# An attention, expert and spatial-gating kernel on one core: first loads reordered, table products and decayed queries of the first chunks moved between engines

## The chip, the cores and the metric

The kernel runs on one core of a Trainium2 chip. The metric is the device time of one execution in microseconds (us), lower is better; the core's engines TensorE, VectorE, ScalarE and GpSimd work side by side, each through its own queue in order, and SyncE (SP) issues most DMAs.

## What is computed

Three stages follow each other: a linear attention with decay, a mixture of experts, and a gated feed-forward with a spatial product. The change touches the attention alone:

```python
def _attn_ref(r, k, v, w, u):                 # B, H, S, D = 2, 8, 768, 48
    state = np.zeros((B, H, D, D))
    for t in range(S):
        kt, vt, rt = k[:, :, t], v[:, :, t], r[:, :, t]
        cur = np.einsum('bhd,bhe->bhde', u[None] * kt, vt)
        y[:, :, t] = np.einsum('bhd,bhde->bhe', rt, state + cur)
        state = w[None, :, :, None] * state + np.einsum('bhd,bhe->bhde', kt, vt)
    return y
...
x = attention.transpose(0, 2, 1, 3).reshape(B, S, H * D)   # then:
# moe: each token goes to one of 8 experts (argmax of x @ w_gate, or the expert of the token before
#      it where a local gate says so); out = p[e] * (relu(x @ w1[e]) @ w2[e])
# moe2: u, v = halves of relu(x @ w_in); out = (u * (w_spatial @ norm(v) + b_spatial)) @ w_out
```

## The kernel before

**Chunks.** The 768 time steps are cut into 6 chunks of 128 (`NC`, `C`), each with 2 batches; I write (c,b) for chunk and batch, and the kernel numbers such halves g = 2c + b. Inside a chunk the recurrence is done as matrix products. A table `rtab` holds the powers of w, `ktab` their reciprocals; queries times `rtab` (tile `rh`) and keys times `ktab` (tile `kt`) give `scores` on TensorE (PSUM tile `pa`, two tiles, one buffer each), `mask` (VectorE) keeps the strictly earlier keys (`am`), and `mix` adds up on TensorE the state of the chunk before (`py` from `st`, L625) and the values under the mask (`py`, L630), after making the new state (`pst`, L614, one PSUM buffer, added into `st` by VectorE, L619, or copied, L621). `prep_keys` makes the keys for the state, `kh` (GpSimd), from `ktok`, the transposed table that `tokens_table` makes: product `one0` (trace: `one`) on VectorE with `wc`, four transposes `pk` on TensorE, a copy on ScalarE.

**Gates and own weights.** `gates` copies v into `vx` on ScalarE, has TensorE multiply it with the gate weights (`gated`, tile `pg`, one PSUM buffer; for (0,0) the buffer `py0`) and copies `pg` into `vx` on ScalarE. `diag` is a generator of three steps: k times u (L546) and times r (L548) on GpSimd (`ku`), and the sum of these over each head on VectorE (`ad`, L551). `own` multiplies `vx` by `ad`, eight instructions on ScalarE (`av`, L567); `own_gates`, `logits` and `rows` read it on VectorE. `decay` multiplies the state by `wc` on ScalarE (L599).

**Order.** The whole is written under a manual schedule: each engine works its instructions off in the order in which the program issues them, and waits on semaphores where one needs another's result or buffer. So the order of the calls in L701 to L748, and in the loop from L748 on (c = 1 to 4), is the order of each queue. `warm` (L101) issues products of constants on TensorE before the first data are there.

**Loads.** `load(c, names, b)` issues one DMA a tensor, for one batch or both, all on SP's queue; the tiles have two buffers a name. Chunk 0 and chunk 1 are issued at L428 to L438, chunk 2 in L725, chunks c + 2 in the loop. `kT`, `rT`, `vT` hold channels in the partitions, `k`, `r`, `v` time steps. `wgb` are the gate weights, `ub` is u for all partitions.

**Who does which product.** `prep` (L503): for (0,0) `powers` makes the tables on VectorE and, in `ready`, two halves of `kt` as the table grows; then GpSimd makes `rh`. Else `kt` is made by VectorE for (0,1), all of chunk 1 and (c,0) of chunks 2 to 4, and by GpSimd otherwise; `rh` is made by GpSimd throughout (L515, L518). `wc` is computed by VectorE at the end of `powers` (L484), `wBad` (a check of w's range) at L736.

Of the kernel before, what the change touches and what calls it, by code (L numbers as in the profile page):

```python
# [16 lines left out]
ALU = mybir.AluOpType  # L17
# [4 lines left out]
B = 2  # L22
# [7 lines left out]
C = 128  # L30
NC = S // C
# [5 lines left out]
G = E + 1  # L37
WS = 3072
LC = D + G
WARM = (16, 9)  # L40
FILL = (3, 0, 0, 7, 0, 1, 0, 5)
WMIN = 0.6
WMAX = 1.1
# [3 lines left out]
def rwkv_moe_gmlp(ctx, tc, a, out):  # L47
# [53 lines left out]
    def warm(ps, tag, n):  # L101

        t = ps.tile([128, 4, 128], F32, name="warm", tag=tag)
        for _ in range(n):
            pe.matmul(t, lhsT=ones, rhs=ones.unsqueeze(1).to_broadcast([128, 4, 128]), start=True, stop=True)
# [301 lines left out]
    with ExitStack() as att:  # L407
# [6 lines left out]
        wT = tp.tile([128, NP], F32, name="wT")  # L414
# [6 lines left out]
        def load(c, names, b=slice(0, B)):  # L421
            t = loads.setdefault(c, {})
            for n in names:
                if n not in t:
                    t[n] = ld.tile(shapes[n], F32, name=n, tag=n)
                sy.dma_start(out=t[n][:, b], in_=a[n][c, :, b])

        wgb = tp.tile([128, 3, H * G], F32, name="wgb")  # L428
        sy.dma_start(out=wgb, in_=a["wgb"])
        load(0, ["vT", "rT", "kT"], 0)  # L430
        load(0, ["vT", "rT", "kT"], 1)
        load(0, ["v", "k"])
        ub = tp.tile([128, H, D], F32, name="ub")
        sy.dma_start(out=ub.rearrange("t h d -> t (h d)"), in_=a["u"].partition_broadcast(128))
        load(0, ["r"])
        for b in range(B):
            load(1, ["kT", "rT", "vT"], b)
        load(1, ["v", "k", "r"])  # L438

        zero = tp.tile([128, DM], F32, name="zero")  # L440
        st = [tp.tile([128, B, NP, C], F32, name=f"st{i}") for i in range(2)]
# [3 lines left out]
        def clear(i):  # L445
            def z(*shape):
                t = zero[:, 0:shape[-1]]
                for _ in shape[:-1]:
                    t = t.unsqueeze(1)
                return t.to_broadcast([128, *shape])  # L450

            v = vx[i].rearrange("t b p a d -> t (b p) a d")
            se.copy(v[:, :, 0, LC:C], z(B * NP, C - LC))
            se.copy(v[:, :, 1, 0:D], z(B * NP, D))
            se.copy(v[:, :, 1, D + LC:C], z(B * NP, C - LC - D))
            se.copy(kh[i][:, :, :, D:64], z(B, H, 64 - D))
            se.copy(st[1 - i].rearrange("t b p d -> t (b p) d"), z(B * NP, C))
# [9 lines left out]
        def powers(ready):  # L467

            ve.memset(one0, 0.0)
            ve.memset(one0[:, :, 0:1], 1.0)  # L470
            ve.memset(wrep[:, :, 0:1], 0.0)

            ve.tensor_scalar(wrep[:, :, 1:C], wT.unsqueeze(2).to_broadcast([128, NP, C - 1]), WMIN, WMAX,
                             op0=ALU.max, op1=ALU.min)
            ve.tensor_tensor_scan(out=flat(rtab), data0=flat(wrep), data1=flat(one0),
                                  initial=0.0, op0=ALU.mult, op1=ALU.add)
            ve.reciprocal(ktab[:, :, 0:16], rtab[:, :, 1:17])
            n = 16
            while n < C:
                ve.tensor_tensor(ktab[:, :, n:2 * n], ktab[:, :, 0:n],  # L480
                                 ktab[:, :, n - 1:n].to_broadcast([128, NP, n]), op=ALU.mult)
                n *= 2
                ready(n)
            ve.tensor_tensor(wc, rtab[:, :, C - 1], wrep[:, :, 1], op=ALU.mult)  # L484

        ktok = tp.tile([128, H, D], F32, name="ktok")

# [15 lines left out]
        def prep(c, b):  # L503

            t = loads[c]
            rh[c, b] = wk.tile([128, NP, C], F32, name="rh", tag=f"rh{b}")
            kt[c, b] = wk.tile([128, NP, C], F32, name="kt", tag=f"kt{b}")
            if c + b == 0:
                def ready(n):
                    o = slice(n // 2, n) if n == C else slice(0, n)  # L510
                    if n >= C // 2:
                        ve.tensor_tensor(kt[0, 0][:, :, o], t["kT"][:, 0, :, o], ktab[:, :, o], op=ALU.mult)

                powers(ready)
                po.tensor_tensor(rh[0, 0], t["rT"][:, 0], rtab, op=ALU.mult)  # L515
                return
            (ve if c * b < 2 and c < NC - 1 else po).tensor_tensor(kt[c, b], t["kT"][:, b], ktab, op=ALU.mult)
            po.tensor_tensor(rh[c, b], t["rT"][:, b], rtab, op=ALU.mult)  # L518

        def prep_keys(c, b=slice(0, B)):  # L520
            k = loads[c]["k"][:, b]
# [3 lines left out]
        def gated(c, b, tag="pg"):  # L525

            pg = ps1.tile([128, H, G], F32, name="pg", tag=tag)
            for k in range(3):
                pe.matmul(pg.rearrange("t h g -> t (h g)"), lhsT=loads[c]["vT"][:, b, k, :],  # L529
                          rhs=wgb[:, k, :], start=(k == 0), stop=(k == 2))  # L530
            return pg
# [47 lines left out]
        def scores(g):  # L579

            c, b = divmod(g, B)
            am[g] = wk.tile([128, 2 * NP, C], F32, name="am", tag="am")
            pa = [ps1.tile([128, NP, C], F32, name="pa", tag=f"pa{h}") for h in range(2)]

            for p in range(NP):
                for h in range(2):
                    pe.matmul(pa[h][:, p, :], lhsT=kt[c, b][64 * h:64 * h + 64, p, :],  # L587
                              rhs=rh[c, b][64 * h:64 * h + 64, p, :], start=True, stop=True)
            am[g, "pa"] = pa
# [109 lines left out]
            sy.dma_start(out=xd[r:r + C, :], in_=x.rearrange("t h d -> t (h d)"))  # L699

        with tc.manual_schedule():  # L701
            warm(ps1, "pz", WARM[0])
            board = Board(ps1, sm)
            pg = gated(0, 0, "py0")
            warm(ps1, "pz", WARM[1])
            prep(0, 0)
            scores(0)
            clear(0)
            tt = tokens_table()
            next(tt)  # L710
# [15 lines left out]
            mask(1)  # L726
            y0 = mix(0)
            prep(1, 0)
            prep(1, 1)
            prep_keys(1)  # L730
            y1 = mix(1)
            next(dg)
            gates(1, 0)
            own(0, 0)
            scores(2)
            ve.tensor_tensor(wBad, wT, wrep[:, :, 1], op=ALU.not_equal)  # L736
            mask(2)
            load(3, ["kT", "rT"])
            own_gates(0, 0)
            logits(0, 0, y0)  # L740
            rows(0, 0, y0)
            gates(1, 1)
            own(0, 1)
            old = rt = iter(())
# [2 lines left out]
            next(dg)  # L747
            for c in range(1, NC - 1):  # L748
                if c + 2 < NC:
                    load(c + 2, [n for n in shapes if n not in loads.get(c + 2, ())])  # L750
                if c < 3:
                    sy.dma_start(out=whole[:, :, 512 * c - 512:512 * c], in_=w_part(0, c - 1))
                if c > 1:
                    w_fetch(*((0, c) if c < NF else (1, 0)))
                next(rt, 0)
                scores(B * c + 1)
                next(dg)
                decay(c, 0)
                mask(B * c + 1)
                prep(c + 1, 0)  # L760
                prep(c + 1, 1)
                if c == 1:
                    own_gates(0, 1)
                    logits(0, 1, y1)
                gates(c + 1, 0)
                decay(c, 1)
                if c + 2 < NC:
                    prep_keys(c + 1)
                next(rt, 0)
                own(c, 0)  # L770
                y0 = mix(B * c)
                rows(c - 1, 1, y1)
                next(rt, 0)
                next(rt, 0)
                own_gates(c, 0)
                scores(B * c + 2)
                gates(c + 1, 1)
                dg = diag(c + 1)
                next(dg)
                next(dg)  # L780
                logits(c, 0, y0)
                rows(c, 0, y0)
                next(old, 0)
                own(c, 1)
                if c == 3:
                    w_split(0, 2, po)

                def selected():
                    next(rt, 0)
                    next(rt, 0)  # L790
                    mask(B * c + 2)

                def ranked():
                    next(rt, 0)
                    next(old, 0)

                y1 = mix(B * c + 1, {0: selected, 2 if c == NF else 3: ranked})
                own_gates(c, 1)
                if c < NF:
                    logits(c, 1, y1)  # L800
                if c == 1:
                    pw_ = ps1.tile([128, NP], F32, name="pwb", tag="pg")
                    pe.matmul(pw_, lhsT=ones, rhs=wBad, start=True, stop=True)
                    ve.tensor_reduce(limit[:, E:E + 1], pw_, axis=AX.X, op=ALU.max)
                if c < NF:
                    old, rt = rt, iter(())
                    if place[c][1] == len(place[c][0]) - 1:
                        g = place[c][0]
                        rt = route(g, board, xr[g, "l"], als[g], sm, ps1)
# [688 lines left out]
```

## Time and profile before

| what | value |
|---|---|
| median of 3 timed runs | 362.3 us (362.19 to 363.47) |
| the profiled execution | 364.96 us |
| its span, first to last instruction | 363.3 us |
| TensorE (PE) busy | 351.5 us, 97% of the span |
| VectorE (DVE) busy | 230.4 us, 63% |
| ScalarE (ACT) busy | 175.8 us, 48% |
| GpSimd (POOL) busy | 171.1 us, 47% |
| mean granted clock of TensorE | 0.990 of full speed |
| attention, experts, spatial stage (by the chain) | 0 to about 80, to about 219, to 363 us |

Times are in us from the start of the span. PE is the matrix product, PEld the weight load that overlaps it. An instruction's duration includes time for which it holds its engine while something blocks it. "[1.59 <-DVE kt L517]" behind an instruction says how long its engine sat idle before it and whose work ended that. The ends of matrix products are modelled, and a group with x16 is 16 instructions from the first start to the last end. L numbers are lines of the kernel.

### The profile page before, as it was taken

To read this page: it belongs to the slowest core of one execution; us is meant where nothing else is said; L and a number is where in the kernel's file an instruction comes from. 1 tells how busy PE (TensorE), PEld (TensorE's weight loads), DVE (VectorE), ACT (ScalarE), POOL (GpSimd) and SP (SyncE) were. 2 spreads that over 40 slices of the span, in tenths; PEclk is the share of its full clock that TensorE was granted. 3 is DMA by queue.
4 is the path that set the end of the run, shared out by engine and by line. 5 is a ranking of instruction groups with operands and counts; after the bars stand their busy time and mean duration, and the time that the engine had idled before them with its cause. 6 is when DMAs were issued, how large, how long until landed. Compare 5 with 4: busy or idle time off the path is not lost.

```text
span 363.3 us, 6486 instructions
## 1 busy us (share of the span) xinstructions
PE 351.5 (97%) x2488; PEld 335.7 (92%) x2488; DVE 230.4 (63%) x428; ACT 175.8 (48%) x344; POOL 171.1 (47%) x106
## 2 busy tenths in 40 slices
PE   8898999999999999999999999999999999999993
PEld 3897999988999999999999999788999999999992
DVE  5867898896569689898988652466787233234000
ACT  4477466652587674746564442345568210102321
POOL 4799993938489773829291023441000522322000
PEclk9998999999999999999999999999999999999997
DMA  6999988233799999988898303436211000000322
GB/s 195 367 405 398 399 266 332 62 114 109 213 357 318 312 334 345 312 275 302 291 307 267 131 1 93 147 95 219 79 19 70 2 0 0 3 0 3 110 87 73
DMA packets 35496, 67.27 MB, mean 185 GB/s; under 512 B 2752, under 2 KB 19392, under 8 KB 35456
## 3 DMA queue, kind: packets, MB, share of 16 engines
q1 hardware_dynamic: 33520, 61.07, 48.8%
q0 software_dynamic: 1792, 5.51, 4.9%
q8 instruction: 21, 0.34, 0.4%
q10 hardware_dynamic: 144, 0.20, 0.2%
q14 instruction: 19, 0.16, 0.1%
HBM read 56.54 MB, written 10.22 MB: 184 GB/s over the span
## 4 chain that ended last, share of the span: by engine, by line
PE 84%; DVE 4%; POOL 4%; DMA 3%; ACT 2%; issue 1%; SPq 0%; POOLq 0%; ACTq 0%; DVEq 0%
PE h L1011 17%; PE o L1061 15%; PE vs L1178 14%; PE po L1194 7%; PE v L1124 7%; PE u L1163 5%; PE py L630 4%; PE pa L587 3%; PE tx L929 2%; PE py L625 2%; PE pst L614 2%; PE pg L529 2%; PE h L1040 2%; DMA kT<-kT 1%; PE o L667 1%
## 5 line engine op out<-in xcount | busy, mean ns | idle before, releaser
L346 POOL TENSOR_TENSOR slot<-raw,slot 128x1536 fp32r<-128x1536 f32 x17 | 61.4, 3612 | 88.8 <-ACT slot L344 88.6
L1011 PE MATMUL h<-xt,slot 128*128 128x256 f32 x504 | 61.7, 284 | 0.0
L1011 PEld LDWEIGHTS h<-xt,slot 128*128 128x128 f32 x504 | 61.3, 192 | 0.1
L1061 PE MATMUL o<-slot,ht 128*128 128x384 f32 x336 | 60.2, 336 | 0.0
L1061 PEld LDWEIGHTS o<-slot,ht 128*128 128x128 f32 x336 | 57.9, 188 | 0.0
L346 DVE TENSOR_TENSOR slot<-raw,slot 128x1536 fp32r<-128x1536 f32 x19 | 42.8, 2253 | 17.4 <-ACT slot L344 17.4
L344 ACT CAST slot<-raw 128x1536 fp32r<-128x1536 f32 x36 | 53.1, 1477 | 0.0
L1178 PE MATMUL vs<-slot,slot 128*128 128x384 f32 x288 | 50.1, 334 | 0.0
L1178 PEld LDWEIGHTS vs<-slot,slot 128*128 128x128 f32 x288 | 49.9, 188 | 0.0
L1185 ACT CAST slot<-gv 128x768 fp32r<-128x768 f32 x8 | 6.7, 837 | 43.9 <-POOL gv L1184 39.4
L1124 PE MATMUL v<-slot,xT 128*128 128x512 f32 x108 | 27.6, 401 | 0.0
L402 POOL DMA_INDIRECT xe<-xd,rowid x16 | 23.7, 1478 | 7.0 <-DVE count L257 3.1
L1184 POOL TENSOR_TENSOR gv<-gv,uT 128x768 f32<-128x768 f32 x7 | 12.9, 1836 | 28.0 <-DVE gv L1182 28.0
L1163 PE MATMUL u<-xT,slot 128*128 128x384 f32 x144 | 25.4, 336 | 0.2 <-ACT uT L1168 0.2
L1163 PEld LDWEIGHTS u<-xT,slot 128*128 128x128 f32 x144 | 25.0, 188 | 0.6 <-ACT uT L1168 0.5
L1194 PE MATMUL po<-slot,slot 128*128 128x384 f32 x144 | 25.1, 335 | 0.0
L630 PE MATMUL py<-vx,am 128*128 128x128 f32 x192 | 25.1, 279 | 0.0
L1194 PEld LDWEIGHTS po<-slot,slot 128*128 128x128 f32 x144 | 25.0, 188 | 0.0
L1021 DVE SCALAR_TENSOR_TENSOR ht<-h,ht 128x512 fp32r<-128x512 f32 (+1 forms) x28 | 18.0, 647 | 8.4 <-ACT ht L1020 8.4
L1124 PEld LDWEIGHTS v<-slot,xT 128*128 128x128 f32 x108 | 19.5, 189 | 3.7
L919 POOL DMA_INDIRECT xg<-ys,slots x12 | 12.0, 1000 | 23.1 <-DMA ys<-ob 14.7
L630 PEld LDWEIGHTS py<-vx,am 128*128 128x128 f32 x192 | 22.9, 192 | 0.0
(205 smaller groups left out, 553.7 us busy)
## 6 DMA issues: line engine op xcount, KB each, us to landing
raw<-w SPq DMA_DIRECT2D x30, 768.0 KB, 6.5
raw<-w_in SPq DMA_DIRECT2D x6, 768.0 KB, 6.3
ys<-ob SPq DMA_DIRECT2D x15, 192.0 KB, 5.0
v<-v SPq DMA_DIRECT2D x6, 384.0 KB, 6.9
k<-k SPq DMA_DIRECT2D x6, 384.0 KB, 7.4
r<-r SPq DMA_DIRECT2D x6, 384.0 KB, 7.7
xd<-x SPq DMA_DIRECT2D x12, 192.0 KB, 3.4
raw<-w_out SPq DMA_DIRECT2D x3, 768.0 KB, 4.5
```

What stands on the lines that cost most here:

```text
L344: se.copy(hi, r)
L346: (eng or ve).tensor_tensor(lo, r, hi, op=ALU.subtract)
L402: po.indirect_dma_start(out=xe[e][:, m], out_offset=None, in_=xd[0:rows_read], in_offset=bass.IndirectOffsetOnAxis(ap=rowid[:, m, e:e + 1] ...
L630: pe.matmul(y[:, p], lhsT=m[:, h * NP + p, :], rhs=v[:, b, p, h, :], start=(c + p + h == 0), stop=(p == NP - 1 and h == 1))
L1011: pe.matmul(h[:, j], lhsT=w1[:, s, k, 128 * f:128 * f + 128], rhs=xt[e][:, m, k], start=(n == 0), stop=(n == 8))
L1021: ve.scalar_tensor_tensor(lo, x, 0.0, hi, op0=ALU.max, op1=ALU.subtract)
L1061: pe.matmul(o, lhsT=hidden(e, m, s, f), rhs=w2[:, q, f], start=(n == 0), stop=(n == 23))
L1124: pe.matmul(o, lhsT=xT[b][:, s, k, 128 * c:128 * c + 128], rhs=win[:, q, k, DF:FF], start=(n == 0), stop=(n == 8))
L1163: pe.matmul(o[:, h, 0:HS], lhsT=win[:, s, k, 128 * d:128 * d + 128], rhs=xT[b][:, q, k, HS * h:HS * h + HS], start=(n == 0), stop=(n == 8))
L1178: pe.matmul(o[:, h, 0:HS], lhsT=vn[b][:, s, k, 128 * d:128 * d + 128], rhs=wsp[q][:, k, HS * h:HS * h + HS], start=(n == 0), stop=(n == 17))
L1184: (ve if b == 1 and d == 3 else po).tensor_tensor(t, t, uT[b][:, d], op=ALU.mult)
L1194: pe.matmul(o, lhsT=gt[b][:, s, k, 128 * c:128 * c + 128], rhs=wout[q][:, k], start=(n == 0), stop=(n == 11))
```

## The change

The first loads come in the order wT, kT and rT of (0,0), wgb, vT of (0,0), then kT, rT, vT of (0,1); chunk 1 is loaded whole, without a split by batch, and kT, rT, vT of chunk 5 are split. `wc` is computed right behind the scan. `rh` of (0,0), (0,1), (1,0), (1,1) and (2,0) is made by VectorE, the rest stays with GpSimd; who makes `kt` is the same as before in another form. 24 warming products come in one piece and `gated(0, 0)` behind `scores(0)`. The sum `ad` of chunk 0 is made between the products of (1,0) and (1,1), `own(0, 0)` stands ahead of `gates(1, 0)`, `wBad` behind `rows(0, 0)`, and the sum `ad` of chunk 1 behind mask(3) and the products of chunk 2.

```diff
--- before.py
+++ after.py
@@ -37,7 +37,7 @@
 G = E + 1
 WS = 3072
 LC = D + G
-WARM = (16, 9)
+WARM = 24
 FILL = (3, 0, 0, 7, 0, 1, 0, 5)
 WMIN = 0.6
 WMAX = 1.1
@@ -425,17 +425,16 @@
                     t[n] = ld.tile(shapes[n], F32, name=n, tag=n)
                 sy.dma_start(out=t[n][:, b], in_=a[n][c, :, b])
 
+        load(0, ["kT", "rT"], 0)
         wgb = tp.tile([128, 3, H * G], F32, name="wgb")
         sy.dma_start(out=wgb, in_=a["wgb"])
-        load(0, ["vT", "rT", "kT"], 0)
-        load(0, ["vT", "rT", "kT"], 1)
+        load(0, ["vT"], 0)
+        load(0, ["kT", "rT", "vT"], 1)
         load(0, ["v", "k"])
         ub = tp.tile([128, H, D], F32, name="ub")
         sy.dma_start(out=ub.rearrange("t h d -> t (h d)"), in_=a["u"].partition_broadcast(128))
         load(0, ["r"])
-        for b in range(B):
-            load(1, ["kT", "rT", "vT"], b)
-        load(1, ["v", "k", "r"])
+        load(1, list(shapes))
 
         zero = tp.tile([128, DM], F32, name="zero")
         st = [tp.tile([128, B, NP, C], F32, name=f"st{i}") for i in range(2)]
@@ -474,6 +473,7 @@
                              op0=ALU.max, op1=ALU.min)
             ve.tensor_tensor_scan(out=flat(rtab), data0=flat(wrep), data1=flat(one0),
                                   initial=0.0, op0=ALU.mult, op1=ALU.add)
+            ve.tensor_tensor(wc, rtab[:, :, C - 1], wrep[:, :, 1], op=ALU.mult)
             ve.reciprocal(ktab[:, :, 0:16], rtab[:, :, 1:17])
             n = 16
             while n < C:
@@ -481,7 +481,6 @@
                                  ktab[:, :, n - 1:n].to_broadcast([128, NP, n]), op=ALU.mult)
                 n *= 2
                 ready(n)
-            ve.tensor_tensor(wc, rtab[:, :, C - 1], wrep[:, :, 1], op=ALU.mult)
 
         ktok = tp.tile([128, H, D], F32, name="ktok")
 
@@ -512,10 +511,9 @@
                         ve.tensor_tensor(kt[0, 0][:, :, o], t["kT"][:, 0, :, o], ktab[:, :, o], op=ALU.mult)
 
                 powers(ready)
-                po.tensor_tensor(rh[0, 0], t["rT"][:, 0], rtab, op=ALU.mult)
-                return
-            (ve if c * b < 2 and c < NC - 1 else po).tensor_tensor(kt[c, b], t["kT"][:, b], ktab, op=ALU.mult)
-            po.tensor_tensor(rh[c, b], t["rT"][:, b], rtab, op=ALU.mult)
+            else:
+                (ve if (c < 2 or b == 0) and c < NC - 1 else po).tensor_tensor(kt[c, b], t["kT"][:, b], ktab, op=ALU.mult)
+            (ve if 2 * c + b < 5 else po).tensor_tensor(rh[c, b], t["rT"][:, b], rtab, op=ALU.mult)
 
         def prep_keys(c, b=slice(0, B)):
             k = loads[c]["k"][:, b]
@@ -699,12 +697,11 @@
             sy.dma_start(out=xd[r:r + C, :], in_=x.rearrange("t h d -> t (h d)"))
 
         with tc.manual_schedule():
-            warm(ps1, "pz", WARM[0])
+            warm(ps1, "pz", WARM)
             board = Board(ps1, sm)
-            pg = gated(0, 0, "py0")
-            warm(ps1, "pz", WARM[1])
             prep(0, 0)
             scores(0)
+            pg = gated(0, 0, "py0")
             clear(0)
             tt = tokens_table()
             next(tt)
@@ -726,19 +723,19 @@
             mask(1)
             y0 = mix(0)
             prep(1, 0)
+            next(dg)
             prep(1, 1)
             prep_keys(1)
             y1 = mix(1)
-            next(dg)
+            own(0, 0)
             gates(1, 0)
-            own(0, 0)
             scores(2)
-            ve.tensor_tensor(wBad, wT, wrep[:, :, 1], op=ALU.not_equal)
             mask(2)
             load(3, ["kT", "rT"])
             own_gates(0, 0)
             logits(0, 0, y0)
             rows(0, 0, y0)
+            ve.tensor_tensor(wBad, wT, wrep[:, :, 1], op=ALU.not_equal)
             gates(1, 1)
             own(0, 1)
             old = rt = iter(())
@@ -747,6 +744,9 @@
             next(dg)
             for c in range(1, NC - 1):
                 if c + 2 < NC:
+                    if c + 2 == NC - 1:
+                        load(c + 2, ["kT", "rT", "vT"], 0)
+                        load(c + 2, ["kT", "rT", "vT"], 1)
                     load(c + 2, [n for n in shapes if n not in loads.get(c + 2, ())])
                 if c < 3:
                     sy.dma_start(out=whole[:, :, 512 * c - 512:512 * c], in_=w_part(0, c - 1))
@@ -754,12 +754,14 @@
                     w_fetch(*((0, c) if c < NF else (1, 0)))
                 next(rt, 0)
                 scores(B * c + 1)
-                next(dg)
+                if c > 1:
+                    next(dg)
                 decay(c, 0)
                 mask(B * c + 1)
                 prep(c + 1, 0)
                 prep(c + 1, 1)
                 if c == 1:
+                    next(dg)
                     own_gates(0, 1)
                     logits(0, 1, y1)
                 gates(c + 1, 0)
```

## Rows read from the trace of the kernel before

**Rows 1.** Busy us, share of the span and instructions, from the page.
```profile
PE 351.5 (97%) x2488; PEld 335.7 (92%) x2488; DVE 230.4 (63%) x428; ACT 175.8 (48%) x344; POOL 171.1 (47%) x106
```
**Rows 2.** Timeline of TensorE: start, us, engine, line, instruction, [idle before, releaser].
```profile
1.13 5.24 PE L105 MATMUL warm<-ones 128*128 128x512 bf16 x16 [1.13 <-DVE ones L71]
6.20 0.79 PE L529 MATMUL pg<-wgb,vT 128*128 128x72 f32 x6
6.83 2.11 PE L105 MATMUL warm<-ones 128*128 128x512 bf16 x9
9.52 1.16 PE L587 MATMUL pa<-rh,kt 64*128 64x128 f32 x16 [0.59 <-DVE kt L512]
...
12.63 1.66 PE L587 MATMUL pa<-rh,kt 64*128 64x128 f32 x16
...
21.50 0.89 PE L529 MATMUL pg<-wgb,vT 128*128 128x72 f32 x6
...
30.16 1.16 PE L587 MATMUL pa<-rh,kt 64*128 64x128 f32 x16 [1.59 <-DVE kt L517]
```
**Rows 3.** Windows: length, PE busy (instructions), PEclk (granted clock), DMA share, GB/s.
```profile
29.00:30.00 1.00, 0.00 (x0) 1.00 1.02 407
...
32.00:33.00 1.00, 1.00 (x6) 0.50 1.03 397
```
**Rows 4.** The chain of work that ended last: start, us, what.
```profile
2.67 5.39 DMA kT<-kT
...
37.40 1.09 PE pa L587 x16
...
39.30 0.33 PE pz L186 x4
...
43.34 1.09 PE pa L587 x16
```
**Rows 5.** Timeline of VectorE.
```profile
8.16 0.42 DVE L512 TENSOR_TENSOR kt<-kT,ktab 128x256 f32<-128x256 f32 x1 [1.40 <-DMA kT<-kT]
...
9.29 1.26 DVE L484 TENSOR_TENSOR wc<-rtab,wrep 128x4 f32<-128x4 f32 x1
10.59 0.69 DVE L489 TENSOR_TENSOR one<-ktab,wc 128x512 f32<-128x512 f32 x1
...
16.93 2.30 DVE L517 TENSOR_TENSOR kt<-kT,ktab 128x512 f32<-128x512 f32 x1
...
20.09 0.95 DVE L551 TENSOR_REDUCE ad<-ku 128x16 f32<-128x768 f32 x1
...
27.05 0.95 DVE L551 TENSOR_REDUCE ad<-ku 128x16 f32<-128x768 f32 x1 [3.12 <-POOL ku L548]
...
37.67 0.20 DVE L167 TENSOR_TENSOR board<-board,als 128x36 f32<-128x36 f32 x1
```
**Rows 6.** Timeline of GpSimd.
```profile
9.26 1.26 POOL L518 TENSOR_TENSOR rh<-rT,rtab 128x512 f32<-128x512 f32 x1 [1.38 <-DMA rT<-rT]
12.58 1.96 POOL L522 TENSOR_TENSOR kh<-k,ktok 128x384 f32<-128x384 f32 x2 [2.05 <-ACT ktok L494]
14.50 1.82 POOL L546 TENSOR_TENSOR ku<-k,ub 128x768 f32<-128x768 f32 x1
16.39 2.28 POOL L548 TENSOR_TENSOR ku<-ku,r 128x768 f32<-128x768 f32 x1
```
**Rows 7.** Timeline of ScalarE.
```profile
21.07 1.97 ACT L567 ACTIVATE av<-vx,ad 128x57 f32<-128x57 f32 x8 [0.29 <-DVE ad L551]
22.95 0.50 ACT L536 COPY vx<-v 128x384 f32<-128x384 f32 x1
23.48 0.23 ACT L538 COPY vx<-pg 128x72 f32<-128x72 f32 x1
```
**Rows 8.** SP issues k of chunk 1; below it that DMA's time from issue to landing.
```profile
14.07 0.33 SPq L426 DMA_DIRECT2D k<-k  x1
...
k<-k SPq DMA_DIRECT2D x1, 384.0 KB, 6.4
```

## Prediction, made before the changed kernel was run

> **What bounds the kernel now.** I read the busy shares first: TensorE works 97% of the span [rows 1], so a change can only bring what TensorE idles or does at a lower clock. Its timeline says where that is: idle stretches ahead of scores(0) (0.59 us) and of scores(4), the first scores of chunk 2 (1.59 us, the largest of the whole run, ended by VectorE's kt), and a scores(1) of 1.66 us where scores(0) took 1.16, so 0.5 of it is waiting [rows 2]. The windows show what followed the 1.59: TensorE did nothing from 29 to 30, and from 32 to 33 its granted clock was 0.50, that is 1.2 instead of 2.4 GHz [rows 3]. The chain of waits gives the price: scores(4) to scores(5) is 37.40 - 30.16 = 7.24; the next half chunk is 43.34 - 37.40 = 5.94 with 0.33 of routing in it. At full clock the first would have been about 5.6; the low clock cost 1.6 [rows 2, 4]. From there the chain is nearly all TensorE. So the question is when scores(4) starts, and at what clock its neighbourhood runs.
>
> Why is scores(4) late? VectorE sat idle 3.12 ahead of ad(1), waiting for GpSimd's ku; mask(3) and kt(2,0) queue behind ad(1) [rows 5]. GpSimd worked without a pause from 12.58, when ktok let its kh begin [rows 6].
>
> I write (c,b) for chunk and batch; scores and masks are numbered 2c+b.
>
> **The start.** kt(0,0) waited 1.40 for kT, issued at 2.67 and landed 5.39 later [rows 4, 5]. In first place kT is issued near 1.3. The wgb and vT that stood there (300 KB) had landed by 6.20, when TensorE read them without a wait [rows 2]; so 256 KB land by then at the latest, and VectorE needs them at 8.16 - 1.40 = 6.76. The 1.40 goes. wc moves forward; it took 1.26, nearly all of it behind GpSimd's rh(0,1), which began at 9.26 and took as long [rows 5, 6]. Behind the scan GpSimd is idle, so its price lies between 0 and the 0.20 of a 36-column product [rows 5]; I take 0.20. kt(0,0) then begins at 6.96, and where wc stood before (1.13 on) VectorE can begin rh(0,0): 8.09. That is an addition: 0.69, as the product of the same size at 10.59 [rows 5]. scores(0) starts 0.15 behind it, at 8.93 instead of 9.52. The 24 warming products end at about 6.4 + 8 x 0.23 = 8.2 [rows 2], ahead of it, so they cost nothing.
>
> VectorE goes on with one, kt(0,1) and rh(0,1) at about 0.65 each: mask(0) starts at 10.7. TensorE does scores(0) to 10.1 and, now in this place, pg(0,0) (0.79) to 10.9; only then the table's transposes. From the end of one to kh there were 12.58 - 11.28 = 1.30 [rows 5, 6], so kh starts at about 12.15, 0.43 earlier. TensorE gains more: 0.4 at scores(1) and its 0.5 of waiting.
>
> **Chunk 1: turns between VectorE and GpSimd.** The second kt of chunk 1 took 2.30 instead of 0.69: it started at 16.93, while GpSimd's ku ran from 16.39, and ended 0.56 after that (16.39 + 2.28 = 18.67). That ku itself took 2.28, not 1.82, having waited 0.46 for the first kt [rows 5, 6]. So such products take turns. The Trainium skill, GPSIMD Engine Reference, section Specifications, says that GpSimd's SBUF interfaces are shared with VectorE and contended when VectorE's instruction has two SBUF inputs; this speaks against the change, whose rh have two, and the trace agrees with its 2.30. Without any contention ad(0) below would come 0.9 earlier and the forecast would be 360.1; the row decides, and I keep the turns.
>
> GpSimd: kh 1.92, ku 1.82, to 15.9; then kt(1,0) has a turn, then ku times r, to 18.67 - 0.43 = 18.24. rh(1,0), now VectorE's, waits for that and ends at 18.8; ad(0) takes 0.95, own(0,0) can start at 19.8. So of the two rh that GpSimd loses in chunk 1 (1.26 each [rows 6]) VectorE makes good use only in part.
>
> own(0,0) now stands ahead of gates(1,0) on ScalarE. Queued behind it are the copies of v and pg; own took 1.88 to the next start (21.07 to 22.95), the copy of v 0.53 to the next start and that of pg 0.23 [rows 7]. pg(1,0) is thus copied out at 19.8 + 1.88 + 0.53 + 0.23 = 22.4, and pg(1,1), which uses the same PSUM buffer, can start only then: at 22.45, against 21.50 before [rows 2]. TensorE is there at 21.50 - 0.9 = 20.6: a **new wait of 1.8 us**. Before, pg(1,1) to the end of mix(2) was 28.57 - 21.50 = 7.07, with 0.5 of waiting for mask(2) that now goes. TensorE is through at 22.45 + 6.57 = 29.0.
>
> **The other way to scores(4).** ad(1) no longer stands ahead of mask(3), so the 3.12 is off this path; kt(2,0) and the added rh(2,0) are on it. GpSimd cannot begin kh(1) before k(1) lands, 14.07 + 6.4 = 20.5 [rows 8]; the bytes ahead of it in the queue are the same as before. kt(1,1) and rh(1,1) follow ad(0) to 21.0; kh(1) takes the next turn, and three of 1.82 end at 26.5; kt(2,0) 27.0; GpSimd's kt(2,1) 1.27, 28.3; rh(2,0) 28.85. Both ways meet at **29.0, 1.15 us before the old 30.16**.
>
> Moves at nothing: wBad behind rows, where a lost turn lies ahead of mask(3) but ends with GpSimd's second ku, some 0.5 before mask(3) is needed; uncovered it costs up to 1.8. ad(1) behind rh(2,0): own(1,0) and the adds into st come later; mix(3) waits about 0.25 for the PSUM buffer, if TensorE is at full clock. Whole loads of chunk 1 make kt(1,0) wait for 512 KB, hidden behind ku. The three more DMA issues for chunk 5 lie in SP's queue some 15 us ahead of use. The relief of GpSimd in chunk 2 is off the path.
>
> **Sum and clock.** The old wait of 1.59 was followed by the low clock. The new one of 1.8 is of that size, with TensorE as busy around it, so I take it that the clock falls again, now within chunk 1, at the same 1.6. Nothing then waits long at scores(4), and no second fall comes. Old and new fall cancel: scores(4) 29.0 + 1.6 = 30.6, scores(5) 36.2 against 37.40, a gain of 1.2; up to 0.3 of the low stretch lies beside waits that are there anyway. Gain 1.3. The profiled execution took 364.96 with a span of 363.3, of which 1.3 would leave 363.7 and 362.0; the median of the timed runs, 362.3, is 2.7 below it, and I take the gain from that: **361.0**. Its own bounds (wc, the turn of kt(1,0), the 0.3) are +-0.8: 360.2 to 361.8.
>
> **Rivals.**
> - *The clock stays up.* The new wait is followed by the low clock in nothing that the trace shows yet, and shorter idle stretches (0.59 at 9.5) were not. Then scores(5) comes at 29.0 + 5.6 + 0.25 = 34.85, a gain of 2.6: 359.7. The timed runs of before spread by 1.3 us, which may be the same thing the other way round.
> - *Lost turns: slower.* rh(2,0) reaches scores(4) with 0.15 to spare, so each further turn that VectorE loses on this path is paid in full. If k(1) lands before 20.3, kh(1) goes ahead of rh(1,1): 1.6 later, 362.6, already slower than before. If then mask(3) ends behind GpSimd's ku, kt(2,0) or rh(2,0) loses one more: 364.2. It decides at k(1)'s landing; 20.5 speaks against it, narrowly.
> - *It brings nothing.* The loads hold chunk 1 anyway: k(1) is 20.5 whatever GpSimd is relieved of, and if whole loads land 1 us later than their halves did, ad(0) and pg(1,1) slip by as much and the gain is gone: 362.3.
>
> **How the numbers follow.** Forecast 0.43, clock up 0.32, lost turns 0.13 (0.08 for one, 0.05 for two), nothing 0.12. The range reaches from below the second to above one lost turn: 359.2 to 363.0. A measurement of this kernel tells about 0.5% (1.8 us) from no change. Faster than 360.5: nearly all of the second and a fifth of the first, 0.40; slower than 364.1: two lost turns and a little, 0.06; between, 0.54.
>
> **What would show it.** scores(0) near 8.9 with no wait for kT; kh at 12.1; ad(0) ending near 19.8; TensorE waiting before pg(1,1), ended by ScalarE's copy at 22.4; scores(4) near 29.0 and no wait of VectorE ahead of mask(3); a granted clock of 0.50 for about 3 us somewhere from 24 on (forecast) or none (rival). I am wrong if ad(0) is done before 18 (own(0,0) then ends before pg(1,0) is there, and nothing waits at pg(1,1)), or if TensorE stops somewhere behind 37.

## The result: 367.0 us against 362.4, and the profile after

The changed kernel takes **367.01 us** (365.80 to 367.75) against 362.4 of the kernel before; the ratio is 1.0106, with an interval of 1.0068 to 1.0143. It is slower by about 1.1%, where 361.0 was forecast.

| | before | after |
|---|---|---|
| median of timed runs | 362.4 us | 367.01 us |
| traced execution, its span | 364.96, 363.3 us | 365.80, 363.5 us |
| TensorE, VectorE, GpSimd busy | 351.5, 230.4, 171.1 us | 353.0, 231.7, 165.0 us |

The two traced executions lie only 0.8 apart: of the 80 executions of the kernel before that were run beside the experiments, 58 had a mean granted clock of 0.994 or more and a median of 362.4 us, and 22 had 0.992 or less and a median of 364.7; the traced one, at 0.990, is like the latter, and all four of the changed kernel had 0.981 to 0.988.

The waits of TensorE in the changed kernel (engine, tile and line, what ended it: us, times, longest):

```profile
PE pg L527 <- ACT vx L536: 2.0, 1, 2.0
...
PE pa L585 <- DVE rh L516: 0.4, 1, 0.4
```

The wait of 1.59 ahead of scores(4) [rows 2] is gone, and a new one of 1.96 stands ahead of pg(1,1), ended by ScalarE. TensorE's timeline (columns as in rows 2):

```profile
8.74 1.16 PE L585 MATMUL pa<-rh,kt 64*128 64x128 f32 x16 [0.38 <-DVE rh L516]
...
22.13 1.56 PE L527 MATMUL pg<-wgb,vT 128*128 128x72 f32 x6 [1.96 <-ACT vx L536]
23.62 2.08 PE L585 MATMUL pa<-rh,kt 64*128 64x128 f32 x16
...
26.97 2.01 PE L612 MATMUL pst<-vx,kh 128*128 128x128 f32 x8
...
33.22 1.16 PE L585 MATMUL pa<-rh,kt 64*128 64x128 f32 x16
...
38.75 1.16 PE L585 MATMUL pa<-rh,kt 64*128 64x128 f32 x16
```

pg(1,1) took 1.56 where a pg took 0.89 [rows 2], and pst 2.01. The windows say why (length, PE busy, PEclk, DMA share, GB/s):

```profile
21.00:22.00 1.00, 0.00 (x0) 1.00 1.04 415
22.00:23.00 1.00, 0.87 (x4) 0.52 1.01 399
...
27.00:28.00 1.00, 1.00 (x6) 0.50 1.00 398
...
31.00:32.00 1.00, 1.00 (x7) 0.50 1.04 402
...
33.00:34.00 1.00, 1.00 (x17) 1.00 1.02 372
```

The granted clock fell at the end of the wait and stayed at 0.50 to a little after 32, about 10 us, with TensorE busy in every one of these windows. In the kernel before it was low for about 3, from shortly before 32 [rows 3] to shortly after 35:

```profile
34.00:35.00 1.00, 1.00 (x6) 0.50 1.02 367
35.00:36.00 1.00, 1.00 (x11) 0.93 1.05 388
```

scores(5), at 37.40 before [rows 4], is at 38.75.

What ended the wait can be read along ScalarE and VectorE (timelines), and from SP's issue of k of chunk 1 with that DMA's time to landing:

```profile
19.44 1.97 ACT L565 ACTIVATE av<-vx,ad 128x57 f32<-128x57 f32 x8 [3.96 <-DVE ad L549]
21.32 0.50 ACT L534 COPY vx<-v 128x384 f32<-128x384 f32 x1
21.85 0.23 ACT L536 COPY vx<-pg 128x72 f32<-128x72 f32 x1
```

```profile
15.64 2.31 DVE L515 TENSOR_TENSOR kt<-kT,ktab 128x512 f32<-128x512 f32 x1 [0.73 <-DMA kT<-kT]
17.87 0.68 DVE L516 TENSOR_TENSOR rh<-rT,rtab 128x512 f32<-128x512 f32 x1
18.47 0.94 DVE L549 TENSOR_REDUCE ad<-ku 128x16 f32<-128x768 f32 x1
19.33 0.68 DVE L515 TENSOR_TENSOR kt<-kT,ktab 128x512 f32<-128x512 f32 x1
19.93 0.68 DVE L516 TENSOR_TENSOR rh<-rT,rtab 128x512 f32<-128x512 f32 x1
...
21.47 1.29 DVE L591 TENSOR_TENSOR am<-pa,upst 128x512 f32<-128x512 f32 x2
```

```profile
19.90 2.38 POOL L520 TENSOR_TENSOR kh<-k,ktok 128x768 f32<-128x768 f32 x1 [2.51 <-DMA k<-k]
```

```profile
10.53 0.33 SPq L426 DMA_DIRECT2D k<-k  x1
...
k<-k SPq DMA_DIRECT2D x1, 384.0 KB, 9.3
```

own(0,0) began when ad(0) was there, the copies of v and pg of (1,0) came behind it, and pg(1,1) behind these. GpSimd's kh(1) is seen to begin 0.03 ahead of rh(1,1) and yet took 2.38, where a product of that size took 1.81 or 1.82 otherwise, and rh(1,1) its plain 0.68: here VectorE still had the turn.

### The profile page after: what moved, and what is told of

Same layout as the page of the kernel before. It is cut to its first block, busy times and chain, and to the rows that moved or that the text cites. A ratio compares the mean times of both kernels' runs of the same rounds, so it can differ in the third digit from the quotient of the medians.

```text
span 363.5 us, 6477 instructions
## 1 busy us (share of the span) xinstructions
PE 353.0 (97%) x2487; PEld 337.7 (93%) x2487; DVE 231.7 (64%) x433; ACT 175.7 (48%) x344; POOL 165.0 (45%) x101
## 4 chain that ended last, share of the span: by engine, by line
PE 86%; DMA 4%; DVE 4%; ACT 2%; SPq 2%; issue 1%; POOL 0%; POOLq 0%; ACTq 0%
PE h L1013 17%; PE o L1063 15%; PE vs L1180 14%; PE po L1196 7%; PE v L1126 7%; PE u L1165 5%; PE py L628 4%; PE pa L585 3%; PE py L623 2%; PE pg L527 2%; PE tx L931 2%; PE pst L612 2%; DMA kT<-kT 2%; PE h L1042 2%; SPq L426 1%
## 5 line engine op out<-in xcount | busy, mean ns | idle before, releaser
L628 PE MATMUL py<-vx,am 128*128 128x128 f32 x192 | 25.9, 285 | 0.0
L565 ACT ACTIVATE av<-vx,ad 128x57 f32<-128x57 f32 x88 | 21.7, 331 | 5.5 <-DVE ad L549 5.5
L628 PEld LDWEIGHTS py<-vx,am 128*128 128x128 f32 x192 | 23.8, 199 | 0.0
```

The source lines that it names most:

```text
L565: se.mul(av[c, b][:, h], v[:, b, h // 2, h % 2, o:o + LC], ad[c][:, b, h:h + 1])
L628: pe.matmul(y[:, p], lhsT=m[:, h * NP + p, :], rhs=v[:, b, p, h, :], start=(c + p + h == 0), stop=(p == NP - 1 and h == 1))
```

## Experiments

All times are medians; ratios are to the kernel before, run on the same chip beside each.

**e1: ScalarE's order put back.**

```diff
-            own(0, 0)
             gates(1, 0)
+            own(0, 0)
```


> The changed kernel, with own(0,0) put back behind gates(1,0) on ScalarE; all else of the change stays. Theory (the new wait of TensorE ahead of pg(1,1) lets the clock fall for 9.6 us): pg(1,0) is copied out near 19.5, TensorE waits at most about 1.2 us for mask(2) instead of 1.96 for the copy, the clock stays up or is low only shortly, and the time is 361 us, a little below before. Rival (the products moved to VectorE lose turns against GpSimd and the whole loads land late, which holds chunk 1 and 2 whatever ScalarE's order): 366 to 367 us as with the whole change.

366.57 us, ratio 1.0124 (1.0093 to 1.0155): as slow as the whole change. The wait moved one step on:

```profile
PE pa L585 <- DVE am L591: 2.6, 1, 2.6
```

```profile
19.70 2.29 DVE L516 TENSOR_TENSOR rh<-rT,rtab 128x512 f32<-128x512 f32 x1
22.02 0.80 DVE L619 COPY st<-pst 48x228 f32<-48x228 f32 x2
22.85 1.29 DVE L591 TENSOR_TENSOR am<-pa,upst 128x512 f32<-128x512 f32 x2
```

```profile
19.21 2.23 POOL L520 TENSOR_TENSOR kh<-k,ktok 128x768 f32<-128x768 f32 x1 [1.45 <-DMA k<-k]
21.41 2.25 POOL L544 TENSOR_TENSOR ku<-k,ub 128x768 f32<-128x768 f32 x1
```

Here k(1) landed earlier, kh(1) began at 19.21 and had the turn ahead of rh(1,1), which took 2.29; mask(2) came at 22.85 instead of 21.47, and TensorE waited 2.6 for it. The clock was at 0.50 from 23 to near 30:

```profile
23.00:24.00 1.00, 0.40 (x2) 0.51 1.01 393
24.00:25.00 1.00, 1.00 (x9) 0.50 1.05 411
```

ScalarE's order alone is not the fault: behind it lies the lost turn of VectorE. It is not e1's edit that brought kh(1) forward: in the traces of e2 and f1, which leave ScalarE's order as changed, kh(1) began at 19.23 and 19.00. When k(1) lands differs from trace to trace.

**e2 and f1: the waits kept, TensorE busy in them.** e2 has the first of these two additions to the changed kernel, f1 both.

```diff
             scores(2)
+            warm(ps1, "pz", 8)
...
+                if c == 1:
+                    warm(ps1, "pz", 5)
                 scores(B * c + 1)
```


> The changed kernel with eight more products of constants (512 columns, 0.21 us each) on TensorE between scores(2) and pg(1,1), where it waits 1.96 us; the wait itself, ScalarE's order and VectorE's stay. Theory (the clock, not the wait, makes the kernel slow): pg(1,1) starts at 22.1 as before, the granted clock stays 1.00, scores(4) starts near 29.0 instead of 33.2 and the time is 361 us. Rival (the moved work itself costs): 366 to 367 us.

> The changed kernel with products of constants on TensorE in both of its waits in chunk 1: eight ahead of pg(1,1) and five ahead of scores(3), where e2 still waited 0.82 us for mask(2). Theory (the clock makes the difference of 4.5 us; the moved work as such is worth about nothing): no execution has a long low clock, and the time is 362.5 to 363.3 us in nearly all of them. Rival (the moved work costs by itself): 365 us or more with the clock up.

e2: 366.74 us (1.0056 to 1.0131), but in two groups: three executions at 362.9 to 363.4 with a mean clock of 0.995 and more, five at 366.7 to 367.8 with 0.985 to 0.992. The trace is of the first group: pg(1,1) at 21.87, scores(4) at 29.70 (29.0 had been worked out), a wait of 0.82 left ahead of scores(3), and the clock never low:

```profile
PE pa L585 <- DVE am L591: 0.8, 1, 0.8
```

```profile
23.00:24.00 1.00, 0.42 (x2) 1.00 1.01 394
27.00:28.00 1.00, 1.00 (x11) 1.00 1.02 401
```

No execution of the second group was traced, so how long TensorE waited in those is not known; f1 fills the place that e2 left open. f1, with the second wait filled too: **363.40 us**, ratio 1.0008 (0.9984 to 1.0032), all ten executions between 362.95 and 364.35 with a clock of 0.995 and more. So with the clock up nearly four fifths of the loss is gone (367.01 - 363.40 = 3.6 of 4.6). The rest of the change, which f1 keeps, gains nothing: the ratio is taken against all executions beside it, low clocks included, and against the 362.4 of those at full clock f1 is 1.0 slower. In f1's trace VectorE's last two products of chunk 1 lost their turns (kt(1,1) 2.29 and rh(1,1) 2.30), and TensorE still waited 1.4 at scores(3), behind the five products put there, with the clock up:

```profile
PE pa L585 <- DVE am L591: 1.4, 1, 1.4
```

```profile
24.00:25.00 1.00, 0.00 (x0) 1.00 1.04 410
27.00:28.00 1.00, 1.00 (x10) 1.00 0.94 307
```

**e3: ScalarE's order alone, in the kernel before.**

```diff
-            gates(1, 0)
             own(0, 0)
+            gates(1, 0)
```


> The kernel before with one edit of the change alone: own(0,0) ahead of gates(1,0) on ScalarE. Theory: pg(1,1) starts near 23.8 instead of 21.5, TensorE waits 2.2 us ahead of it, the clock falls there, and the time is 364 to 367 us. Rival (a wait alone, much of it taken from the 1.59 us that TensorE waited at scores(4) anyway): no more than 363.2 us.

366.43 us, ratio 1.0113 (1.0067 to 1.0160). By itself this edit does as much harm as the whole change:

```profile
PE pg L529 <- ACT vx L538: 2.2, 1, 2.2
```

```profile
22.00:23.00 1.00, 0.00 (x0) 1.00 1.00 395
24.00:25.00 1.00, 1.00 (x7) 0.50 1.05 407
32.00:33.00 1.00, 1.00 (x6) 0.50 1.04 392
```

**h1: the two products of chunk 1 back on GpSimd, ScalarE's new order kept.**

```diff
-            (ve if 2 * c + b < 5 else po).tensor_tensor(rh[c, b], t["rT"][:, b], rtab, op=ALU.mult)
+            (ve if c == 0 or (c, b) == (2, 0) else po).tensor_tensor(rh[c, b], t["rT"][:, b], rtab, op=ALU.mult)
```


> The changed kernel with rh(1,0) and rh(1,1) back on GpSimd; own(0,0) stays ahead of gates(1,0), and all else of the change stays. Theory (each of the two, ScalarE's order and the two products on VectorE, is enough by itself to stop TensorE in chunk 1 for over a microsecond and let the clock fall): pg(1,1) still waits for ScalarE's copy of pg(1,0), about 1.5 us, and the time is 365 to 367 us. Rival (the two products on VectorE are the whole fault, since ad(0) comes earlier without them): 361.5 to 362.5 us.

361.79 us, ratio 0.9962 (0.9936 to 0.9988). My theory fell here: within the changed kernel, putting back these two products is enough. Without them ad(0) starts at 17.75 instead of 18.47, and mask(2) at 20.36:

```profile
PE pg L527 <- ACT vx L536: 1.3, 1, 1.3
```

```profile
17.75 0.95 DVE L549 TENSOR_REDUCE ad<-ku 128x16 f32<-128x768 f32 x1 [1.70 <-POOL ku L546]
18.62 0.87 DVE L515 TENSOR_TENSOR kt<-kT,ktab 128x512 f32<-128x512 f32 x1
...
20.36 1.29 DVE L591 TENSOR_TENSOR am<-pa,upst 128x512 f32<-128x512 f32 x2
```

```profile
21.00:22.00 1.00, 0.57 (x5) 1.00 1.05 418
22.00:23.00 1.00, 1.00 (x9) 0.67 0.99 389
27.00:28.00 1.00, 1.00 (x6) 0.50 1.00 394
```

The wait of 1.26 that ScalarE's order leaves was followed by a low clock in the traced execution (363.80 us, mean clock 0.988), but eight of the ten have 0.995 or more. So what VectorE does later than before lengthens the wait from one that is mostly harmless to one (1.96) behind which all four executions had a low mean clock.

**f4: all five products to VectorE, alone.**

```diff
-                po.tensor_tensor(rh[0, 0], t["rT"][:, 0], rtab, op=ALU.mult)
+                ve.tensor_tensor(rh[0, 0], t["rT"][:, 0], rtab, op=ALU.mult)
...
-            po.tensor_tensor(rh[c, b], t["rT"][:, b], rtab, op=ALU.mult)
+            (ve if 2 * c + b < 5 else po).tensor_tensor(rh[c, b], t["rT"][:, b], rtab, op=ALU.mult)
```


> The kernel before with one part of the change alone: rh of (0,0), (0,1), (1,0), (1,1) and (2,0) on VectorE. Theory (turns): VectorE's products wait behind GpSimd's ku and kh, mask(2) comes 0.5 to 1.5 us later than 21.6, TensorE waits for it at scores(3) for over 1 us and the clock falls in part of the executions: 364 to 366 us. Rival (the order of ScalarE alone was the fault): 361.5 to 362.5 us.

364.73 us, ratio 1.0048 (1.0025 to 1.0071); the mean clock was between 0.985 and 0.993 in eight of ten. Two waits, the larger one at scores(4), where rh(2,0) lost its turn:

```profile
PE pa L587 <- DVE rh L518: 1.9, 1, 1.9
...
PE pa L587 <- DVE am L593: 1.0, 2, 0.8
```

The traced execution (363.71 us, mean clock 0.995) is one of the two others: behind a wait of 1.92, as long as that of the changed kernel, its clock stayed at 1.00. The length of a wait alone does not decide.

```profile
30.00:31.00 1.00, 0.00 (x0) 1.00 1.05 403
32.00:33.00 1.00, 1.00 (x14) 1.00 1.04 399
```

**e4: the old wait filled.** Seven such products ahead of scores(4) in the kernel before.

```diff
+                if c == 1:
+                    warm(ps1, "pz", 7)
                 scores(B * c + 2)
```


> The kernel before with seven more products of constants (0.21 us each) on TensorE ahead of scores(4), where it waits 1.59 us. If the low clock seen from 32 to 35 us in its profile is also in its timed executions, it goes with the wait filled: 360.8 us. If the timed executions ran at full clock anyway, the time stays at 362.4 us.

362.28 us, ratio 0.9995 (0.9958 to 1.0032), the traced execution at 361.91 with no low clock in chunk 2. The timed executions of the kernel before mostly ran at full clock: there was little to win back at the place where I had counted a cancelled 1.6. The trace shows one thing more. Its loads are those of the kernel before, yet kT of (0,0) landed 3.4 us after its issue instead of 5.39 [rows 4], kt(0,0) starts at 7.39 without waiting for it, and scores(0) at 8.75, as early as in the changed kernel. In e3 and g2, with the same loads, kT took 4.5 and 4.1 us and kt(0,0) did not wait for it either. So the 1.40 [rows 5], too, belongs to the one execution that the prediction was read from.

**f3, g2: the loads alone; the later sum alone** (the lines are those of the change).

> The kernel before with the new order of loads alone (keys and queries of (0,0) first, chunk 1 whole, chunk 5 split). Theory (the loads only start chunk 0 earlier; GpSimd's chain from ktok on still sets scores(4)): 361.5 to 362.5 us, kt(0,0) not waiting. Rival (whole loads are late for chunk 1 and open a wait at scores(2), with the clock falling): 364 us or more.

> The kernel before with one part of the change alone: the sum ad(1) behind mask(3) and the products of chunk 2. Theory: the wait of 1.59 ahead of scores(4) shrinks to what GpSimd's rh(2,0) leaves (it ended at 28.2 against 28.57 of TensorE), so scores(4) starts near 28.6 instead of 30.2, the clock falls in no execution, 361.0 to 361.4 us. Rival (VectorE's kt(2,0) loses its turn to GpSimd's products of chunk 2 and the wait stays): 362.3 us.

f3: 361.95 us, ratio 0.9974 (0.9946 to 1.0002); scores(4) still waits 1.60, but starts at 29.36. g2: 361.95 us, 0.9973 (0.9942 to 1.0004). There scores(4) starts at 29.47 with no wait ahead of it; in the traced execution 1.45 of it came back ahead of scores(3), where mask(2) was late behind wBad, itself held by GpSimd (1.18); g2's edit touches nothing ahead of that, so it is the turns of that one execution. Both are a little faster at best; neither is settled.

**f5 and g1: the start kept, chunk 1 left as it was.** f5 has rh(1,0), rh(1,1), ad(0), own(0,0) and the loads of chunk 1 as before; g1 also has rh(2,0) on GpSimd and wBad ahead of mask(0), but loads chunk 1 whole. Of g1 against the changed kernel:

```diff
-            (ve if 2 * c + b < 5 else po).tensor_tensor(rh[c, b], t["rT"][:, b], rtab, op=ALU.mult)
+            (ve if c == 0 else po).tensor_tensor(rh[c, b], t["rT"][:, b], rtab, op=ALU.mult)
...
+            ve.tensor_tensor(wBad, wT, wrep[:, :, 1], op=ALU.not_equal)
             mask(0)
...
             prep(1, 0)
-            next(dg)
             prep(1, 1)
             prep_keys(1)
             y1 = mix(1)
-            own(0, 0)
+            next(dg)
             gates(1, 0)
+            own(0, 0)
...
             rows(0, 0, y0)
-            ve.tensor_tensor(wBad, wT, wrep[:, :, 1], op=ALU.not_equal)
```


> The changed kernel without its parts in chunk 1: rh(1,0) and rh(1,1) on GpSimd, ad(0) and own(0,0) in the old places, chunk 1 loaded by batch. The new start, rh of (0,0), (0,1), (2,0) on VectorE and ad(1) behind the products of chunk 2 stay. Theory: chunk 1 has no wait of over 1 us, scores(4) starts near 28.3, the clock stays up, 360.7 to 361.5 us. Rival (GpSimd's chain is as long as before and the wait at scores(4) as large): 362.3 us.

> The changed kernel with rh of chunks 1 and 2 on GpSimd as before, ad(0) and own(0,0) in the old places, and wBad ahead of mask(0), before GpSimd begins kh. The new loads, the new start with rh(0,0) and rh(0,1) on VectorE and ad(1) behind the products of chunk 2 stay. Theory (what was good in the change is the start and mask(3) no longer behind ad(1); what was bad is each product of chunks 1 and 2 taken to VectorE beside a busy GpSimd): scores(4) starts near 27.7, no wait of TensorE over 0.6 us in chunk 1, 361.0 to 361.5 us. Rival (f5 had it all): 361.9 us.

f5: 361.96 us, ratio 0.9968 (0.9945 to 0.9991). g1: **361.77 us**, ratio 0.9965 (0.9940 to 0.9991), all executions at a clock of 0.994 and more:

```profile
PE pa L585 <- POOL rh L516: 0.6, 2, 0.4
```

```profile
28.10 1.16 PE L585 MATMUL pa<-rh,kt 64*128 64x128 f32 x16 [0.24 <-POOL rh L516]
```

scores(4) starts at 28.10 with TensorE waiting 0.24, against 30.16 [rows 2]. Not all of the 2 us is a gain: the median is 0.8 lower, and in e4's trace, with the loads of the kernel before and a clock that stayed up, scores(4) started at 29.31. Both are a little faster than the two kernels compared here: by 0.4 (f5) and 0.6 us (g1) against the 362.4 of the kernel before at full clock. Neither can be told from the other, nor from h1.

## Why the prediction was wrong, by its steps

| step | worked out | in the trace after |
|---|---|---|
| scores(0), kh | 8.93, 12.15 | 8.74, 11.76 |
| kt(1,0) | a turn ahead of ku times r | lost it: kT landed 15.6, 2.31 |
| ad(0), own(0,0) start | 18.8, 19.8 | 18.47, 19.44 |
| wait ahead of pg(1,1), its end | 1.8, 22.45 | 1.96, 22.13 |
| kh(1) starts | 21.0 | 19.90 |
| low clock | 3 us, costs 1.6 | about 10 us, costs 4.5 |
| scores(4), scores(5) | 30.6, 36.2 | 33.22, 38.75 |

**Right:** the price of a lost turn, and the new wait with its place, length and cause. Up to 22.1 no time is off by more than 0.4 except kh(1). Some of that is luck: which product lost the turn ahead of ad(0) came out the other way, at the same price. The start came as worked out, but the gain there was counted against one execution: e4 has scores(0) as early with the old loads. The list of TensorE's idle stretches left out 0.65 us ahead of the table's transposes (pk), ended by VectorE's one; it is gone as well.

**Wrong: "Sum and clock".** I let the old and the new fall of the clock cancel at 1.6 each. Neither size held. The new one: from pg(1,1) to scores(4) I had counted 6.57 at full clock; it took 33.22 - 22.13 = 11.09, so the low clock cost 4.5. That it lasts three times as long as the one seen before, with TensorE busy throughout, is nothing a row of the kernel before showed, and my bounds had no end for it. The old one: I took the gain from the median of the timed runs, but the 1.6 was in the traced execution, and in most timed ones not (e4, and 58 of the 80 executions beside the experiments). I had written that the median lies 2.7 below the traced execution and did not ask why; the low clock was in that difference. So in the median there was no old fall to cancel the new one. Put right by these rows, scores(5) comes at 36.2 + 2.9 = 39.1 against 37.40 - 1.6 = 35.8, and the kernel takes about 362.3 + 3.3 = 365.6 us, an estimate. The traced execution took 365.80; the other three took 0.5 to 2.0 more at a higher mean clock (0.985 to 0.988 against 0.981), which the low clock does not explain. None of them was traced, so that part stays open. The gain without the clock did not come either: f1, with the clock up, is at 363.4, not below 362.4.

**The rival "clock up"** named the right quantity and the wrong side. It read the spread of the timed runs as a sign that shorter waits may be harmless; that was so for the wait that the change removed, not for the one it made.

**The rival "lost turns"** came true in part. k(1) landed at 10.53 + 9.3 = 19.8, not at 20.5, so "the same bytes ahead" did not fix its time; it now stands behind fewer DMA issues, but that this is the reason is not shown. In e1 and e2 kh(1) went ahead of rh(1,1), as that rival has it for landings before 20.3: rh(1,1) took the 1.6 more that it names, and mask(2) came 1.4 later. In f1, where k(1) landed first of all, kt(1,1) lost its turn as well. In the trace of the changed kernel it was a matter of 0.03 us. It priced the turns without the clock.

**Left unweighed:** the wait that each of the two ways makes is enough on its own. e1 takes one away and finds the other; h1 takes VectorE's and shortens the first as well.

## What to carry to other kernels

A wait of TensorE has two prices, its length and what the clock does behind it, and a change that only moves a wait can pay the second anew; before counting a low clock as won back, look whether the timed executions had it at all (their mean clock) and not the traced one alone. The same goes for a wait for a load. Work taken off a busy GpSimd is not worth its time when VectorE has to take it with two SBUF inputs beside that same GpSimd: in these traces it could wait for the turn (2.3 us instead of 0.68), and what queues behind it waits too. A short copy that frees a buffer for TensorE should not stand behind long work of the same engine.

## What the runs showed of the hardware

- **The clock after a wait.** TensorE stood 1.96 (after), 2.19 (e3) and 2.59 us (e1) in chunk 1, and all four executions of each had a mean clock of 0.990 or less. At 0.992 or less were 22 of 80 after 1.59 (before), one of ten after 1.60 (f3) and after 1.45 (g2), and two of ten after 1.26 (h1). After 1.92 at scores(4), with 0.78 at scores(3) ahead of it (f4), it was seven of ten, but not the traced one. Each wait is that of the traced execution. The low stretches in the traces lasted about 3 us (before), 7 (e1, h1) and 10 us (after, e3), with TensorE at work again for all or nearly all of them. What sets their length, and which waits are followed by one, these runs leave open.
- **Time outside the span.** The kernels with rh(1,0) and rh(1,1) on VectorE took 1.98 to 2.39 us more than their span in every execution (after, e1, e2, f1, f4), all others 1.66 to 1.88. For the changed kernel that is about 0.4 of the loss, and for f1 about 0.5, that no row of the trace holds; its cause was not looked for.
